# A sequence transform by eight products of 95 rows and 95 columns instead of seven of up to 128 by 377, on one Trainium2 core

## The chip, the cores and the metric

One core of one Trainium2 chip runs the whole program. The metric is the device time of one execution in microseconds (us). Most executions of a kernel agree within 0.3%. A program on one core can show single slow runs; every run quoted here was of the fast state, and the kernel before was run on the same chip in the same rounds as each kernel it is compared with. "Same" means within 2%. Engines: PE is the tensor engine, PEld its weight loads, DVE the vector engine, ACT the scalar engine, POOL is GpSimd.

## The reference

```python
def setup_inputs():            # float32; w_in and w_out reach the kernel as float64
    x = randn(8, 3008, 256) * 0.1
    w_in = randn(256, 2048) / sqrt(256)
    w_out = randn(2048, 256) / sqrt(2048)

def reference(x, w_in, w_out):
    X = np.fft.fft(np.fft.fft(x, axis=1), axis=2).real     # along the sequence (3008), then the features (256)
    h = X.reshape(8 * 3008, 256) @ w_in
    return np.maximum(0.01 * h, h) @ w_out                 # leaky ReLU
```

## The kernel before

The feature transform is folded into w_in, and w_out's seven-product scheme is made once. What remains for each of 8 batches is the sequence transform, then the up-products (`cos_ps`, `sin_ps`), the leaky ReLU and the down-products (`sum_ps`). Frequencies are taken by parity (c = 1 or 0), and each (batch, parity), called a unit, has two parts, cosine and sine. A unit feeds 24 steps, each with four up-products and seven down-products. The folding of x (mirrored rows and columns added and subtracted) runs on DVE. The transform of one part was four products into one bank and three into another, of 95 or 128 rows and 188 to 377 columns:

```python
def even_rows(rows, m, part, c):                 # 4 products of 95 rows
    pe, kf = dft_ps(), KF[c]
    for i in range(NI[0]):
        ... nc.tensor.matmul(to, lhsT=still, rhs=tab[0:PE_ROWS, at : at + to.shape[1]], ...)
def odd_rows(rows, m, part, c):                  # 3 products of 128 rows
    ... nc.tensor.matmul(to, lhsT=still, rhs=tab[:, at : at + to.shape[1]], ...)

def butterfly(t, sums, m, part, c):              # one ACT copy, four DVE operations
    pe, po = sums
    nc.scalar.copy(e0[0:m, 0:kf], pe[0:m, 0:kf])
    nc.vector.tensor_tensor(ev[0:m, 0:kf], e0[0:m, 0:kf], pe[0:m, kf : 2 * kf], op=ALU.add)
    nc.vector.tensor_tensor(ev[0:m, kf:kw], *((x, y), (y, x))[part], op=ALU.subtract)
    nc.vector.tensor_tensor(t[0:m, 0:kw], ev[0:m, 0:kw], po[0:m, 0:kw], op=ALU.add)
    nc.vector.tensor_tensor(t[0:m, kw : UW[c]], ev[0:m, 0:rest], po[0:m, 0:rest], op=ALU.subtract)
```

The start fixes the order of DVE and PE by hand: x of batch 0 comes in four pieces, is folded, transformed, and the first up-products follow, while w_in and w_out are converted from float64 on DVE and ACT. Column d = 128 of x travels apart, as one row of 8 batches ("the d = 128 row", `nyq`). After step 16 the scheduler orders the engines by itself. `keep_warm(n)` issues n products of zeros that only keep the tensor engine busy.

Of the kernel before, what the change touches and what calls it, by code (L numbers as in the profile page):

```python
# [57 lines left out]
NI = [4, 3]  # L59
NT = 7  # L60
PE_ROWS = 95

PO_ROWS = 60
# [4 lines left out]
KF = [189, 188]  # L68
KP = [1, 0]

TW = [[4 * PE_ROWS, 2 * KW[0]], [4 * KF[1], 3 * KW[1]]]
# [12 lines left out]
def m_order(r):  # L84



    at = np.arange(P)[:, None]
    if r == 0:
        m = np.concatenate([2 * at, 2 * at + 1, 376 - 2 * at, 375 - 2 * at], axis=1)  # L90
        last = np.array([188, 187, 190, 189])
        return np.where(at < PE_ROWS - (last != 188), m, -1)
    half = at // (P // 2)
    m = P + at % (P // 2)
    m = np.where(at % (P // 2) < PO_ROWS, np.where(half, 375 - m, m), -1)
    return np.concatenate([at, 375 - at, m], axis=1)


def k_order(c):

    k = 2 * np.arange(KF[c])[::-1] + c
    return np.concatenate([k, Q - k[KP[c] :]])


def laid_out(x):



    m = np.concatenate([m_order(0), m_order(1)], axis=1)
    rows = 2 * m + np.repeat([0, 1], NI)  # L110
    d = np.concatenate([np.arange(P + 1), np.arange(D - 1, P, -1)])
    x = np.concatenate([x, np.zeros((B, 1, D), x.dtype)], axis=1)

    def taken(rows, d):
        return x[:, np.where(m < 0, S, rows % S)][..., d]

    mirrored = (D - d) % D
    x = np.stack([
        np.stack([taken(rows, d), taken(S - rows, mirrored)], axis=2),
        np.stack([taken(H - rows, d), taken(H + rows, mirrored)], axis=2),  # L120
    ], axis=2)
    nyquist = x[..., P].transpose(1, 2, 3, 4, 0).copy()
    x[..., P] = 0.0
    return x, nyquist


def seq_tables():


    out = np.zeros((4, 2, P, TW[1][1]), np.float32)  # L130

    def values(m, r, c):

        s, k = 2 * m + r, k_order(c)
        weight = np.where(m < 0, 0.0, np.where((s == 0) | (s == Q), 0.5, 1.0))[:, :, None]
        turn = (s[:, :, None] * k) % S
# [6 lines left out]
    for r in range(2):  # L143
        for part, t in enumerate(values(m_order(r), r, 1)):
            if r == 0:
                t = t[:, :, : KF[1]]
            out[2 * part + r, 1, :, : TW[1][r]] = t.reshape(P, -1)
    for part, t in enumerate(values(m_order(0), 0, 0)):
        for q in range(2):
            for p in range(2):  # L150
                v = t[:, q, p : KF[0] : 2]
                at = (2 * q + p) * PE_ROWS
                out[2 * part, 0, :, at : at + v.shape[1]] = v

    m = m_order(1)
    m[P // 2 :, 2] = m[: P // 2, 2]
    difference = np.arange(P)[:, None] // (P // 2)
    for part, t in enumerate(values(m, 1, 0)):
        last = t[:, 2] * ((np.arange(KW[0]) + part) % 2 == difference)
        out[2 * part + 1, 0, :, : TW[0][1]] = np.concatenate([t[:, 0, 0::2], t[:, 0, 1::2], last], axis=1)  # L160
    return out

# [28 lines left out]
def columns():  # L191

    at = np.zeros(B * S, np.int64)
    for b, c, j, n, first in chunks()[0]:
        col = j + np.arange(n)
        half = col >= KW[c]
        k = k_order(c)[np.where(half, col - KW[c], col)]
# [7 lines left out]
def tile_fnet_leaky_relu(  # L205
# [6 lines left out]
    seq_tab: bass.AP,  # L212
    feat_tab: bass.AP,
# [29 lines left out]
    def fold_columns(t, h, part, rows):  # L243
# [4 lines left out]
        else:  # L248
            nc.vector.tensor_tensor(z[:, :, P + 1 : D], a[:, :, 1:P], a[:, :, P + 1 : D], op=ALU.subtract)
            nc.gpsimd.memset(z[:, :, P : P + 1], 0.0)  # L250

    def fold_halves(t, part, c, rows, to=None):
# [4 lines left out]
        nc.vector.tensor_tensor(to, z[:, 0], z[:, 1], op=(ALU.add, ALU.subtract)[i])  # L257

    def fold_x(b):
        t, rows = xs.pop(b), slice(0, NT)  # L260
        for h in range(2):
            add_mirrors(t, h, rows)
            for part in range(2):
                fold_columns(t, h, part, rows)
        for part in range(2):
            for c in PARITIES:
                fold_halves(t, part, c, rows)
        zs[b] = t

    def fold_quarters(src, sums, last, tmp):  # L270


        for op, to in zip((ALU.add, ALU.subtract), sums):
            nc.vector.tensor_tensor(to[0:PE_ROWS, 0:2], src[0:PE_ROWS, 0:2], src[0:PE_ROWS, 2:4], op=op)
            nc.vector.tensor_tensor(to[:, 4], src[:, 4], src[:, 5], op=op)
        lo, hi = slice(0, PO_ROWS), slice(P // 2, P // 2 + PO_ROWS)
        nc.scalar.copy(tmp[0][lo], src[hi, 6])
        nc.scalar.copy(tmp[1][hi], src[lo, 6])
        nc.vector.tensor_tensor(last[lo], src[lo, 6], tmp[0][lo], op=ALU.add)
        nc.vector.tensor_tensor(last[hi], tmp[1][hi], src[hi, 6], op=ALU.subtract)  # L280

    def fold_x_quarters(b, part):

        src, z = zs[b][:, part, 0, :, part * P : (part + 1) * P], zs[b][:, part, 1]
        halves = [z[:, :, i * P : (i + 1) * P] for i in range(2)]
        fold_quarters(src, halves, halves[0][:, 5], [h[:, 6] for h in halves])
        quarters[b, part] = halves, halves[0][:, 5]


    folded = {}  # L290
    quarters = {}
# [7 lines left out]
    nyx = const.tile([P, 2, 2, NT, B], F32, name="nyx")  # L299
    inf = const.tile([P, 2], F32, name="inf")  # L300
# [119 lines left out]
    def even_rows(rows, m, part, c):  # L420



        pe, kf = dft_ps(), KF[c]
        tab, n = tabs[2 * part, c], NI[0]
        for i in range(n):
            if c == 1:
                still, to = rows[0:PE_ROWS, i], pe[0:m, i % 2 * kf : (i % 2 + 1) * kf]
            else:
                q, p = divmod(i, 2)  # L430
                still, to = rows[0][(p + part) % 2][0:PE_ROWS, q], pe[0:m, q * kf + p : (q + 1) * kf : 2]
            at = i * TW[c][0] // n

            nc.tensor.matmul(to, lhsT=still, rhs=tab[0:PE_ROWS, at : at + to.shape[1]],  # L434
                             start=(i == 0), stop=(i == n - 1), skip_group_check=True)
        return pe

    def odd_rows(rows, m, part, c):

        po, kw = dft_ps(), KW[c]  # L440
        tab, n, at = tabs[2 * part + 1, c], NI[1], 0
        for i in range(n):
            if c == 1:
                still, to = rows[:, NI[0] + i], po[0:m, 0:kw]
            elif i < 2:
                still, to = rows[0][(i + part) % 2][:, NI[0]], po[0:m, i:kw:2]
            else:
                still, to = rows[1], po[0:m, 0:kw]
            nc.tensor.matmul(to, lhsT=still, rhs=tab[:, at : at + to.shape[1]],  # L449
                             start=(i == 0), stop=(i == n - 1), skip_group_check=True)  # L450
            at += to.shape[1]
        return po

    def butterfly(t, sums, m, part, c):

        pe, po = sums
# [356 lines left out]
```

## Time and profile before

| | before |
|---|---|
| median of three runs | 1931.69 us (1930.21 to 1931.74) |
| span of the profiled run | 1927.9 us |
| PE, DVE, ACT, POOL busy | 99%, 60%, 24%, 55% |
| granted TensorE clock | 1.000 on the mean |

The prediction shows the lines of the page, of the long middle and of single transforms. One more view is needed later: the stretches view of the start, cut where DVE ends the second mix (the sine part's last additions) of the first unit, about where the first sine product begins (28.90 here). Columns: stretch, its length, busy PE, weight loads, DVE, ACT, POOL (with instructions), granted clock, share of the DMA engines, GB/s.

```profile
8.00:28.62 20.62, 18.40 (x86) 12.55 (x85) 17.43 (x32) 4.13 (x11) 2.56 (x7) 1.00 0.82 323
```

DVE worked for 17.43 of the 20.62 us, GpSimd for 2.56, and the clock was full.

### The profile page before, as it was taken

Reading aid. Unit: us, or ns where it says so; the run is one execution under the profiler, and the core shown is the slowest. Engines: PE = TensorE matmul, PEld = TensorE weight load, DVE = VectorE, ACT = ScalarE, POOL = GpSimd, SP = SyncE. Lnnn points to the kernel's source line nnn. Section 1 sums busy time; section 2 is a strip of 40 time slices with the busy share of each in tenths; the row PEclk is TensorE's granted clock in tenths of the full one; section 3 lists DMA queues with packets and bytes.
Section 4 is the critical chain, followed back from the end, with each engine's and each line's share of the span. In section 5 each row is a group of like instructions: output and inputs, shape, how many; then the busy total and the mean of one; then the engine's idle time right before and its main releaser. Section 6 shows DMA issues by size and latency. Waiting matters only on the chain.

```text
span 1927.9 us, 24851 instructions
## 1 busy us (share of the span) xinstructions
PE 1918.2 (99%) x9060; PEld 1694.9 (88%) x9060; DVE 1156.7 (60%) x2276; ACT 468.4 (24%) x554; POOL 1063.3 (55%) x1515
## 2 busy tenths in 40 slices
PE   9999999999999999999999999999999999999999
PEld 7788888888888888888888888888888888888888
DVE  8868555585555755567545765557654585555554
ACT  3532222222222222222222222222222222222221
POOL 1136555575555755566555665556655575555554
PEclk9999999999999999999999999999999999999999
DMA  6202000110002000020000200002000020000000
GB/s 247 77 31 96 12 20 22 52 55 12 21 21 88 19 12 30 12 95 12 22 20 12 95 22 12 20 12 95 23 11 20 12 106 12 19 11 23 11 12 22
DMA packets 26728, 73.29 MB, mean 38 GB/s; under 512 B 4832, under 2 KB 17760, under 8 KB 24816
## 3 DMA queue, kind: packets, MB, share of 16 engines
q1 hardware_dynamic: 25456, 71.71, 10.0%
q8 instruction: 72, 1.18, 0.2%
q14 instruction: 48, 0.39, 0.1%
q10 hardware_dynamic: 1152, 0.00, 0.0%
HBM read 46.99 MB, written 24.71 MB: 37 GB/s over the span
## 4 chain that ended last, share of the span: by engine, by line
PE 97%; DVE 1%; DMA 1%; ACTq 0%; issue 0%; ACT 0%; SPq 0%; DVEq 0%
PE sum_ps L606 57%; PE cos_ps L543 17%; PE sin_ps L543 17%; PE dft_ps L449 3%; PE sum_ps L586 2%; PE dft_ps L434 2%; DMA xt<-in_x_dram 1%; PE wf_ps L396 0%; DMA feat_sb<-in_feat_tab_dram 0%; DVE cos L548 0%; DVE g L552 0%; ACTq L405 0%; DVE g L553 0%; ACT wf L398 0%; DVE power L361 0%
## 5 line engine op out<-in xcount | busy, mean ns | idle before, releaser
L548 DVE SCALAR_TENSOR_TENSOR cos<-nb,wn,cos_ps 128x251 f32<-128x251 f32 (+1 forms) x768 | 330.5, 472 | 674.3 <-PE cos_ps L543 673.8
L554 ACT ACTIVATE g<-g 128x1004 f32<-128x1004 f32 (+1 forms) x384 | 399.2, 1039 | 1191.7 <-DVE g L553 1094.9
L561 POOL TENSOR_TENSOR s<-g 128x251 f32<-128x251 f32 (+1 forms) x368 | 271.5, 738 | 733.7 <-ACT g L554 733.6
L606 PE MATMUL sum_ps<-s,wt 128*128 128x251 f32 (+1 forms) x2208 | 528.0, 374 | 0.0
L606 PEld LDWEIGHTS sum_ps<-s,wt 128*128 128x128 f32 x2208 | 415.5, 188 | 53.1 <-issue 0.6
L543 PE MATMUL cos_ps<-mix,wf 128*128 128x251 f32 (+1 forms) x1536 | 388.3, 375 | 1.8 <-ACT wf L398 1.8
L543 PE MATMUL sin_ps<-mix,wf 128*128 128x251 f32 (+1 forms) x1536 | 387.8, 374 | 0.0
L606 PE MATMUL sum_ps<-g,wo 128*128 128x251 f32 (+1 forms) x1472 | 371.9, 374 | 0.0
L543 PEld LDWEIGHTS cos_ps<-mix,wf 128*128 128x128 f32 x1536 | 290.9, 190 | 37.4 <-ACT wf L398 2.8
L543 PEld LDWEIGHTS sin_ps<-mix,wf 128*128 128x128 f32 x1536 | 290.4, 189 | 34.7
L606 PEld LDWEIGHTS sum_ps<-g,wo 128*128 128x128 f32 x1472 | 279.3, 190 | 39.3 <-DVE o L617 0.3
L564 POOL TENSOR_TENSOR s<-g,s 128x251 f32<-128x251 f32 (+1 forms) x368 | 272.5, 741 | 28.9
L552 DVE TENSOR_TENSOR g<-cos,sin_ps 128x502 f32<-128x502 f32 (+1 forms) x384 | 259.7, 676 | 47.4 <-DVE cos L548 12.2
L562 POOL TENSOR_TENSOR s<-s,g 128x251 f32<-128x251 f32 (+1 forms) x368 | 275.5, 749 | 0.0
L563 POOL TENSOR_TENSOR s<-g 128x251 f32<-128x251 f32 (+1 forms) x368 | 260.4, 708 | 0.0
L553 DVE TENSOR_TENSOR g<-cos,sin_ps 128x502 f32<-128x502 f32 (+1 forms) x384 | 257.2, 670 | 0.0
L606 PE MATMUL sum_ps<-s,wo 128*128 128x251 f32 (+1 forms) x736 | 215.8, 375 | 0.0
L606 PE MATMUL sum_ps<-g,wt 128*128 128x251 f32 (+1 forms) x736 | 215.8, 375 | 0.0
L606 PEld LDWEIGHTS sum_ps<-s,wo 128*128 128x128 f32 x736 | 139.5, 189 | 16.3
L606 PEld LDWEIGHTS sum_ps<-g,wt 128*128 128x128 f32 x736 | 139.8, 190 | 15.8
L617 DVE TENSOR_TENSOR o<-e,sum_ps 128x251 f32<-128x251 f32 (+1 forms) x184 | 67.4, 408 | 8.7 <-ACT e L615 8.7
L586 PE MATMUL sum_ps<-g,wo 128*128 128x251 f32 x256 | 57.4, 375 | 0.0
(75 smaller groups left out, 680.8 us busy)
## 6 DMA issues: line engine op xcount, KB each, us to landing
xt<-in_x_dram SPq DMA_DIRECT2D x14, 1792.0 KB, 9.0
out_dram<-o SPq DMA_DIRECT2D x80, 251.0 KB, 2.3
raw<-in_w_out_dram SPq DMA_DIRECT2D x8, 512.0 KB, 4.6
out_dram<-o SPq DMA_DIRECT2D x16, 250.0 KB, 2.1
raw<-in_w_in_dram SPq DMA_DIRECT2D x6, 512.0 KB, 4.7
nb<-nyq_dram SPq DMA_DIRECT2D x8, 376.5 KB, 3.3
nb<-nyq_dram SPq DMA_DIRECT2D x7, 376.0 KB
xt<-in_x_dram SPq DMA_DIRECT2D x2, 1024.0 KB, 9.5
```

The costliest lines, as they stand in the source:

```text
L543: nc.tensor.matmul(pt[blk][:, h * n : (h + 1) * n], lhsT=wf[:, blk, fs[h] * P : (fs[h] + 1) * P], rhs=mixed[b, c][blk][:, at : at + n], st ...
L548: nc.vector.scalar_tensor_tensor(cos[:, hs], in0=spreads[b, c][:, at : at + n], scalar=wn[:, fs[h] : fs[h] + 1], in1=pt[0][:, hs], op0=ALU ...
L552: nc.vector.tensor_tensor(g[:, 0], cos[:, 0 : 2 * n], pt[1][:, 0 : 2 * n], op=ALU.add)
L553: nc.vector.tensor_tensor(g[:, 1], cos[:, 0 : 2 * n], pt[1][:, 0 : 2 * n], op=ALU.subtract)
L554: nc.scalar.activation(g, g, ACT.Lrelu)
L561: nc.gpsimd.tensor_tensor(s1, a[1][0], a[1][1], op=ALU.add)
L562: nc.gpsimd.tensor_tensor(s2, s1, a[0][0], op=ALU.subtract)
L563: nc.gpsimd.tensor_tensor(s3, a[0][0], a[1][0], op=ALU.subtract)
L564: nc.gpsimd.tensor_tensor(s4, a[0][1], s2, op=ALU.subtract)
L586: nc.tensor.matmul(sums[j][d][:, r * n : (r + 1) * n], lhsT=wo[:, fs[h] // NH, fs[h] % NH, d * P : (d + 1) * P], rhs=a[r][h], start=(f == ...
L606: nc.tensor.matmul(sums[j][p], lhsT=still[p], rhs=moving[p], start=(f == 0 and i % 2 == 0), stop=(f == NH - 1), skip_group_check=True)
L617: nc.vector.tensor_tensor(to, x, y, op=ALU.add)
```

## The change

The intent is to hold the tensor engine for a shorter time in each transform. Rows of x are sorted into eight chunks of 95 instead of seven of up to 128. Some chunks are first *turned*: pairs of rows are combined with a cosine and a sine (ACT makes two scaled copies, DVE two scalar_tensor_tensor operations, or ACT four copies and GpSimd two additions). After that eight products of 95 rows and some 95 columns give what seven wider ones gave, and a longer *butterfly* (nine operations and two ACT copies instead of four and one) puts the frequencies together. The d = 128 row's butterfly in the start goes to GpSimd, and so do the sine's last folds and turns. x is folded in two halves per batch instead of one. The core of the diff:

```diff
-NI = [4, 3]
-NT = 7
-PE_ROWS = 95
-PO_ROWS = 60
+NI = [4, 4]
+NT = 8
+ROWS = 95
@@
-    def fold_x(b):
+    def fold_x(b, h):
...
+    def turn(x, y, a, part, tmp, to, v):
+        nc.scalar.activation(tmp[0], y, ACT.Copy, scale=sin)
+        nc.scalar.activation(tmp[1], y, ACT.Copy, scale=cos)
+        if v is nc.vector:
+            v.scalar_tensor_tensor(to[0], in0=x, scalar=cos, in1=tmp[0], op0=ALU.mult, op1=op[part])
+            v.scalar_tensor_tensor(to[1], in0=x, scalar=sin, in1=tmp[1], op0=ALU.mult, op1=op[1 - part])
+            return
+        ...                                      # on GpSimd: two more ACT copies, two additions
@@ 
+    def products(stills, to, tab, bank):         # four products into one bank, twice a part
+        for i, (still, o) in enumerate(zip(stills, to)):
+            nc.tensor.matmul(o, lhsT=still, rhs=moving, start=(i == 0), stop=(i == 3), skip_group_check=True)
@@
-    def butterfly(t, sums, m, part, c):
+    def butterfly(to, m, part, c, v=nc.vector):  # parity 1: five operations in even, four in odd
...
@@ steps
-                    if n % 2 == 1:
-                        fold_x(b + 1)
+                if part == 0 and n % 2 == 1 and f in (2, 5):
+                    fold_x(b + 1, f // 5)
@@ start
+            fold_columns(t, 0, 1, evens, nc.gpsimd)
+            nyq = mix_nyquist(nyq, nc.gpsimd)
...
+            cosine.fold_even()
+            sine.fold_even(nc.gpsimd)
...
+            even, odd = mix(units[0], 0)
+            even(even_cosines)
+            fold_halves(t, 1, 1, odds, v=nc.gpsimd)
+            sine.fold_odd(nc.gpsimd)
+            odd_cosines = odd_rows(cosine, P)
+            odd(odd_cosines)
+            spread_first(nyq)
+            even, odd = mix(units[0], 1)
+            even(even_sines)
+            odd(odd_rows(sine, P))
             o.begin()
             o.mantissa()
-            mix(units[0], 1, sums_of_sines)
```

## The prediction

> **What bounds the kernel now.** I read the page first, then the stretches view, then the tensor engine's timelines around single transforms, and the timeline of the first 35 us last. The page and its chain of work that ended last:
>
> ```profile
> PE 1918.2 (99%) x9060; PEld 1694.9 (88%) x9060; DVE 1156.7 (60%) x2276; ACT 468.4 (24%) x554; POOL 1063.3 (55%) x1515
> ...
> PE 97%; DVE 1%; DMA 1%; ACTq 0%; issue 0%; ACT 0%; SPq 0%; DVEq 0%
> PE sum_ps L606 57%; PE cos_ps L543 17%; PE sin_ps L543 17%; PE dft_ps L449 3%; PE sum_ps L586 2%; PE dft_ps L434 2%; DMA xt<-in_x_dram 1%; PE wf_ps L396 0%; DMA feat_sb<-in_feat_tab_dram 0%; DVE cos L548 0%; DVE g L552 0%; ACTq L405 0%; DVE g L553 0%; ACT wf L398 0%; DVE power L361 0%
> ```
>
> The tensor engine is on 97% of the chain, and the transform that the change rewrites (dft_ps, L434 and L449) is only 5% of it as rounded. Busy PE alone proves little, since its ends are modelled, so I look at the long middle by itself:
>
> ```profile
> 200.00:1900.00 1700.00, 1700.00 (x8064) 1511.87 (x8063) 990.27 (x1948) 393.75 (x445) 987.41 (x1407) 1.00 0.08 30
> ```
>
> Columns: length, then busy PE, weight loads, DVE, ACT, POOL, granted clock, DMA share, GB/s. In 1700 us the tensor engine never stands still, DVE and POOL have 42% to spare, DMA 92%. Whatever time the transform's products take there is paid in full; what DVE, ACT, POOL and DMA do is hidden. So the measure of the change is: how long is the tensor engine held by one part (one unit, cosine or sine) before and after. Starts of successive groups tell it, not busy times. First a part of parity 1, then one of parity 0, both PE:
>
> ```profile
> 259.77 1.44 PE L434 MATMUL dft_ps<-tab,xt 95*128 95x188 f32 x8
> 261.04 2.06 PE L449 MATMUL dft_ps<-tab,xt 128*128 128x376 f32 x6
> 262.94 1.01 PE L606 MATMUL sum_ps<-g,wo 128*128 128x251 f32 x4
> ```
>
> ```profile
> 146.79 1.03 PE L434 MATMUL dft_ps<-tab,xt 95*128 95x95 f32 x8
> 147.66 1.47 PE L449 MATMUL dft_ps<-tab,xt 128*128 128x189 f32 x6
> ```
>
> Every f32 product leaves two records (x8 is four products, x6 is three). Parity 1 holds the engine from 259.77 to 262.94, 3.17 us. Parity 0 starts at 146.79 and the next product of another kind starts at 148.96: 2.17 us. The wide products show the price of a column: six records of 376 in 1.90 us, 317 ns each, 0.84 ns per column and record. The narrow ones break that price: 8 records of 95 columns should take 8 x 80 ns = 0.64 us, and took 0.87 us (109 ns each). The weight-load row and a warming group of 126 columns say why:
>
> ```profile
> 11.66 2.19 PEld L651 LDWEIGHTS sum_ps<-blank 128*128 128x128 f32 x18
> ```
>
> Eighteen loads of about 0.19 us each in 2.19 us: one starts every (2.19 - 0.19)/17 = 0.118 us on the average, and their matmuls (126 columns, 18 in 2.17 us, the last 0.275) every (2.17 - 0.275)/17 = 0.111 us. A product of 128 stationary columns is thus never nearer than 0.112 us a record to the next, however few columns it moves. The counter-case is the d = 128 row at 120.92 us: the same 95 columns but 8 stationary ones run 8 records in 0.67 us, 84 ns each, which is the column price.
>
> **What the Trainium skill says.** "TensorE: Matmul & The Clock Gate", section "LDWEIGHTS (loading the stationary operand)": a load lasts P/1.2 ns, P being its columns and not the rows of the contraction; 128 columns give 107 ns. The trace agrees with the pace (112 ns, with 95 rows as with 128), not with the recorded duration (190 ns, loads overlap). The same page, "Back-to-back issue gap": in a stream of load and matmul pairs both set the spacing. Agreed, as above. "VectorE: DVE Perf Modes", section "The TRN2 errata": an fp32 tensor_tensor takes (N+151)/0.96 ns. The trace has 0.54 us for 376 columns, 0.41 for 256, 0.28 for 128: agreed, and small operations are mostly fixed cost. "SBUF — State Buffer", "Who interferes with whom": a DVE tensor_tensor with two SBUF inputs shuts GpSimd out for its whole length. The trace agrees: one GpSimd addition at 156.45 us took 2.17 us beside a 2.02 us DVE addition of 1792 columns, others 0.63.
>
> **The change, part by part.**
>
> *Tensor engine.* A part of parity 1 had 4 x 188 + 3 x 376 = 1880 columns in 7 products; it gets 380 + 378 = 758 in 8. Parity 0 had 378 + 754 = 1132 in 7; it gets 380 + 382 = 762 in 8. By columns (2 x 0.84 ns) the new part would take 1.28 us. I do not take that: all its products have 94 to 96 columns and 128 stationary ones, so 16 records x 0.112 = 1.79 us holds. Parity 1 saves 3.17 - 1.79 = 1.38 us, parity 0 saves 2.17 - 1.79 = 0.38. Batches 1 to 7 of parity 1 (14 parts; batch 0 lies in the start) give 14 x 1.38 = 19.3; 16 parts of parity 0 give 16 x 0.38 = 6.1; the d = 128 row of parity 0, 8 stationary columns, goes from 2.03 us (120.92 to 122.95) to 16 x 0.084 = 1.34, 0.7. Sum **26.1 us**. The dft_ps share of the chain should fall from 4.4% to about 3.1%.
>
> *DVE.* Per batch now: from the groups, folding of x 14.3 us (2 x 2.04, 4 x 1.26, 4 x 1.30), quarters 5.0, butterflies 57.1/8 = 7.1; 26.4. After, with the (N+151)/0.96 that the trace bears out: folding 8/7 as much, 16.3; rows 32 operations of 128 or 256 columns, 10.4; butterflies nine operations a part instead of four, 1880 and 1507 columns, 2 x (3.4 + 3.0) = 12.8. Sum 39.5: 13 us more per batch, about 105 us in all, DVE busy 60% to some 66%. The fold of x, one 14 us lump before, now comes as two halves, which the instruction order shows spread one operation per step between the evacuations. Hidden.
>
> *ACT.* 16 scaled copies and some more evacuations per batch, some 8 us each batch, ACT 24% to 28%. Hidden. *GpSimd:* only the start's folds, hidden later. *DMA:* x is 8/7 as large, tables less than half; DMA is idle in the middle. Hidden.
>
> *The start.* Before, the last piece of x is folded from 18.60 us, and the first real up-product begins at 27.95, sines at 28.90:
>
> ```profile
> 18.60 0.96 DVE L241 TENSOR_TENSOR xt<-xt 128x768 f32<-128x768 f32 x1 [0.30 <-DMA xt<-in_x_dram]
> ...
> 27.95 1.11 PE L543 MATMUL cos_ps<-mix,wf 128*128 128x251 f32 x4
> ```
>
> Bytes ahead of the last piece: before 0.52 (w) + 0.26 (feature table) + 0.11 + 3.67 (x) + 0.96 (two tables) = 5.5 MB; after 0.52 + 0.13 + 4.19 + 0.39 = 5.2. At the 343 GB/s of the first 20 us it lands some 0.8 us sooner, 17.8. Then, in the order that the instruction listing gives: DVE 1.23 + 0.69 + 0.79 to 20.5; ACT's first scaled copies and four DVE turns 1.5, to 22.0; two sums of 256, 0.8; eight products 1.8; a copy 0.3, to 24.9; odd cosines 1.8 to 26.7; sines 1.5 + 1.8 to 30.0, against 28.6 before. So the first sine product comes about 1.4 us later, and the first conversion of w_out, three operations that ran between the two mixes, now comes after them. From 20 to 80 us DVE is 17 to 18 us busy of each 20 and the tensor engine waits about 3 us in all, so a later DVE can cost it. I charge **+1.5 us** (0 to 4).
>
> Time: 1931.7 - 26.1 + 1.5 = **1907 us**, 1.3% faster.
>
> **Rivals.**
> 1. *The column count rules.* Then a part takes 1.28 us and the saving is 14 x 1.89 + 16 x 0.89 + 0.7 = 41 us: 1892, just over 2%. Against it stand the 0.109 and 0.111 us of two groups of 95 and 126 columns.
> 2. *DVE becomes a bound in places.* It gains 13 us a batch in more and smaller operations that wait for ACT and for each other, and the two transform banks come from the same four as the up-products. If the evacuation is late, PE waits. For it: DVE at 66%, and steps where a fold fills the 4.66 us of a step. Against it: before, a 14 us fold cost nothing, and the sums wait three steps behind. If each of 30 parts cost 0.5 us, 1922.
> 3. *GpSimd is shut out longer* by the added SBUF additions and its sums come late. It has 42% spare and some 8 us of lead, so I expect 0 to 3 us.
> 4. *The start gets worse or better* by several us: more links between DVE, ACT, PE and GpSimd, against a shorter first load. 1903 to 1912.
>
> **Range and chances.** The 26 us rest on a measured pace, with 1 to 2 us of doubt at joints between groups; the start has 3 either way; rivals 2 and 3 only lengthen. So 1900 to 1916. Over 2% faster needs 1894 or less: only rival 1, or a start 13 us shorter than I think, 6%. Slower by 2% would take a stall of 60 us, 1%.
>
> **What would show it.** Right: 16 records per part spaced 0.112 us, a transform every 1.8 us for both parities, PE without idle time from 200 to 1900 us, DVE near 66%, the first up-product at 27 to 30 us. Wrong: records at 80 to 90 ns (rival 1); gaps of PE before up-products ended by DVE evacuations of dft_ps or cos_ps (rival 2), or before sum_ps ended by GpSimd (rival 3); PE gaps before 130 us that differ by more than 4 us from the kernel before (rival 4).

## The result and the profile after

| | before | after |
|---|---|---|
| median (four runs each) | 1930.95 us (1929.78 to 1931.74) | 1920.22 us (1919.46 to 1921.36) |
| span of the profiled run | 1927.9 us | 1917.6 us |

The ratio is 0.9945 (95% interval 0.9928 to 0.9963): "same", 0.55% faster. Here and below a ratio is the mean time of one kernel's fast runs over the mean of the other's fast runs of the same rounds, so it is not quite the ratio of the medians. The prediction took off 24.6 us (26.1 less 1.5); about 10 came.

The page of the kernel after, busy times and the chain of work that ended last:

```profile
PE 1898.6 (99%) x9132; PEld 1689.9 (88%) x9132; DVE 1293.5 (67%) x2580; ACT 514.1 (27%) x721; POOL 1136.7 (59%) x1551
...
PE 92%; DVE 4%; issue 1%; DMA 0%; ACTq 0%; ACT 0%; DVEq 0%; SPq 0%
```

DVE at 67% and ACT at 27% are what was predicted (66% and 28%). But PE carries only 92% of the chain instead of 97%, and DVE 4% instead of 1%: in several places the end of the program now hangs on DVE. First, the transform itself, on PE's timeline around one part (start, busy us, engine, line, operation, tiles, shapes, count):

```profile
228.37 1.92 PE L524 MATMUL dft_ps<-tab,xt 95*128 95x95 f32 x16
230.13 1.04 PE L735 MATMUL sum_ps<-g,wo 128*128 128x251 f32 x4
```

From 228.37 to 230.13 is 1.76 us for 16 records, 0.110 us each, where 1.79 were predicted and 3.17 or 2.17 were held before. So the saving is there: 14 x (3.17 - 1.76) + 14 x (2.17 - 1.76) = 25.5 us for the 28 parts of the middle. The stretches view of the middle shows the first leak:

```profile
200.00:1900.00 1700.00, 1696.24 (x8212) 1517.97 (x8211) 1125.52 (x2253) 430.86 (x567) 1049.29 (x1425) 1.00 0.08 32
400.00:800.00 400.00, 398.99 (x1928) 356.74 (x1927) 272.61 (x542) 104.28 (x141) 254.59 (x339) 1.00 0.08 28
```

PE was busy for all 1700 us before; now it misses 3.8 by this view, in six waits in five of the batches, all ended by DVE's L746. (Starts will show 5.4 us below: PE's ends are modelled and hide the first part of each wait.) One such place on PE's timeline, and DVE's timeline in front of it; the brackets name the idle time before a group and what ended it:

```profile
648.64 1.04 PE L735 MATMUL sum_ps<-g,wo 128*128 128x251 f32 x4
650.45 1.09 PE L735 MATMUL sum_ps<-s,wt 128*128 128x251 f32 x4 [0.76 <-DVE e L746]
```

```profile
645.26 1.76 DVE L280 TENSOR_TENSOR xt<-xt 128x1024 f32<-128x1024 f32 x1
...
648.11 0.40 DVE L746 TENSOR_TENSOR o<-e,sum_ps 128x250 f32<-128x250 f32 x1
648.44 0.40 DVE L746 TENSOR_TENSOR e<-e,sum_ps 128x250 f32<-128x250 f32 x1
648.76 1.21 DVE L280 TENSOR_TENSOR xt<-xt 128x1024 f32<-128x1024 f32 x1
649.90 0.73 DVE L746 TENSOR_TENSOR e<-e,sum_ps 128x250 f32<-128x250 f32 x2
```

L746 empties the banks in which the next chunk's down-products begin. L280, the fold of the next batch's x, is nobody's hurry, but it stands between the L746 operations in DVE's queue, 1.21 us long, and PE waits for the one behind it.

The second leak is the start. The stretches view up to the end of DVE's second mix:

```profile
8.00:38.94 30.94, 22.92 (x94) 17.24 (x93) 23.51 (x40) 9.57 (x31) 20.81 (x35) 0.73 0.53 197
20.00:40.00 20.00, 13.28 (x41) 9.57 (x40) 17.65 (x34) 7.77 (x25) 9.69 (x18) 0.59 0.25 81
```

DVE ended that mix at 38.94 instead of 28.62 (the sine product, at 38.63, waited only for its first half). DVE was busy 6.1 us longer (23.51 against 17.43) and stood idle 4.2 us longer; GpSimd worked 20.81 us instead of 2.56; from 20 to 40 us the granted clock was 0.59. DVE's timeline shows where the 10 us arise:

```profile
15.24 1.06 DVE L280 TENSOR_TENSOR differences<-xt 128x512 f32<-128x512 f32 x1
...
19.93 0.69 DVE L280 TENSOR_TENSOR xt<-xt 128x512 f32<-128x512 f32 x1 [1.91 <-POOL xt L273]
20.54 1.22 DVE L264 TENSOR_TENSOR xt<-xt 128x1024 f32<-128x1024 f32 x1
21.79 0.93 DVE L270 TENSOR_TENSOR xt<-xt 128x512 f32<-128x512 f32 x1
22.64 0.93 DVE L272 TENSOR_TENSOR xt<-xt 128x508 f32<-128x508 f32 x1
23.50 1.21 DVE L264 TENSOR_TENSOR xt<-xt 128x1024 f32<-128x1024 f32 x1
24.75 0.69 DVE L270 TENSOR_TENSOR xt<-xt 128x512 f32<-128x512 f32 x1
25.47 1.63 DVE L280 TENSOR_TENSOR differences<-xt 128x512 f32<-128x512 f32 x1
27.57 0.80 DVE L301 SCALAR_TENSOR_TENSOR folded<-differences,angle,folded 95x128 f32<-95x128 f32 x1 [0.47 <-ACT folded L298]
```

The last piece of x is folded from 23.50, not from 17.8, and no bracket there names a DMA: DVE came late, not the data. One operation of 512 columns takes 0.69 us at 19.93 and 1.06 or 1.63 at 15.24 and 25.47, where GpSimd has additions of its own. The wait of 1.91 us is for a memset of four values, which stood in GpSimd's queue behind the d = 128 butterfly. The first up-product begins at 36.52 instead of 27.95.

To follow this shift I read from PE's timeline where the first up-product of the k-th step starts (384 steps: 16 units of 24), "the k-th up-product" for short:

| up-product | before | after | later by |
|---|---|---|---|
| 1st | 27.95 | 36.52 | 8.6 |
| 3rd | 40.68 | 51.89 | 11.2 |
| 16th | 114.16 | 125.39 | 11.2 |
| 25th | 161.21 | 170.75 | 9.5 |
| last (384th) | 1909.86 | 1899.56 | -10.3 |

From the 3rd to the 16th the two kernels run in step, 11.2 us apart. So whatever happens up to the 3rd up-product is paid in full. One caution for what follows: each kernel has one profile, and the first piece of x, for which DVE waits, is folded from 8.9 to 9.9 us in the profiles of this study (9.66 before, 9.01 after). Differences under about one us between two profiles' starts are not settled.

### The profile page after: what moved, and what is told of

The parts are those of the page before. It is cut to its first block, busy times and chain, and to the rows that moved or that the text cites. A ratio compares the mean times of both kernels' runs of the same rounds, so it can differ in the third digit from the quotient of the medians.

```text
span 1917.6 us, 25461 instructions
## 1 busy us (share of the span) xinstructions
PE 1898.6 (99%) x9132; PEld 1689.9 (88%) x9132; DVE 1293.5 (67%) x2580; ACT 514.1 (27%) x721; POOL 1136.7 (59%) x1551
## 3 DMA queue, kind: packets, MB, share of 16 engines
q1 hardware_dynamic: 25600, 74.40, 10.4%
## 4 chain that ended last, share of the span: by engine, by line
PE 92%; DVE 4%; issue 1%; DMA 0%; ACTq 0%; ACT 0%; DVEq 0%; SPq 0%
PE sum_ps L735 54%; PE cos_ps L672 16%; PE sin_ps L672 16%; PE dft_ps L524 3%; PE sum_ps L715 2%; DVE g L681 1%; DVE cos L677 1%; DVE g L682 1%; DVE xt L280 1%; DVE xt L272 0%; DMA xt<-in_x_dram 0%; PE wf_ps L468 0%; DVE xt L264 0%; DVE e L746 0%; ACTq L477 0%
## 5 line engine op out<-in xcount | busy, mean ns | idle before, releaser
L691 POOL TENSOR_TENSOR s<-s,g 128x251 f32<-128x251 f32 (+1 forms) x368 | 318.6, 866 | 0.0
L693 POOL TENSOR_TENSOR s<-g,s 128x251 f32<-128x251 f32 (+1 forms) x368 | 279.7, 760 | 28.9
L746 DVE TENSOR_TENSOR o<-e,sum_ps 128x251 f32<-128x251 f32 (+1 forms) x184 | 67.4, 408 | 8.7 <-ACT e L744 8.7
L524 PEld LDWEIGHTS dft_ps<-tab,xt 95*128 95x128 f32 x484 | 59.2, 192 | 1.6
```

The source lines that it names most:

```text
L524: nc.tensor.matmul(o, lhsT=still, rhs=moving, start=(i == 0), stop=(i == 3), skip_group_check=True)
L691: nc.gpsimd.tensor_tensor(s2, s1, a[0][0], op=ALU.subtract)
L693: nc.gpsimd.tensor_tensor(s4, a[0][1], s2, op=ALU.subtract)
L746: nc.vector.tensor_tensor(to, x, y, op=ALU.add)
```

## The experiments

Names used in the expectations. CLOCK: the tensor engine's halved clock makes the start long. CHAIN: DVE's waits in the start, above all the one for GpSimd's memset, do. PORT: GpSimd's added operations stretch DVE's. OWN WORK: the added operations themselves, by their number, fill DVE's queue. DVE ORDER: the scheduler's order of DVE makes the gaps of the middle. Other names are explained in the expectation that brings them. All kernels are the one after with small edits; a kernel that computes wrong results on purpose is marked, and all others gave correct results.

### 1. The wait for the memset

```diff
             v.tensor_tensor(z[:, :, P + 1 : D], a[:, :, 1:P], a[:, :, P + 1 : D], op=ALU.subtract)
-            nc.gpsimd.memset(z[:, :, P : P + 1], 0.0)
```

> The changed kernel without GpSimd's zeroing of column 128 of the folded rows (the host already sends zeros there, so results stay right). Question: why does the first up-product start at 36.5 us instead of 28. Theory CHAIN (DVE's folding of the first batch is held up, by GpSimd's queue among others): the 1.9 us that DVE waited for GpSimd at 18.0 us disappear, the first up-product starts near 34.5, the whole is about 2 us shorter. Theory CLOCK (the tensor engine runs at half clock from 18.6 to 42.5 us and that makes the start long): no change, within 0.5 us.

Measured: 1918.69 us (1917.73 to 1918.83), ratio to before 0.9935 (0.9918 to 0.9951). The first up-product came at 37.70, 1.2 us *later* (x itself began 0.5 later in this profile); that the median is 1.5 us below after's in spite of it comes from the middle. The wait of 1.91 us is gone, but DVE now ran beside more of GpSimd's work. DVE's timeline of this run:

```profile
24.16 2.45 DVE L270 TENSOR_TENSOR xt<-xt 128x512 f32<-128x512 f32 x1
```

The same operation took 0.69 us at 24.75 above. The wait was not a cost by itself: taken away, it came back as longer operations and the start got no shorter.

### 2. The clock

```diff
-            keep_warm(8)
+            keep_warm(12)
             even_cosines = even_rows(cosine, P)
...
+            keep_warm(4)
             even_sines = even_rows(sine, P)
+            keep_warm(12)
```

> The changed kernel with more warming products on zeros where the tensor engine stood idle in the start (12 instead of 8, then 4 and 12 more). Theory CLOCK: the granted clock stays 1.0 from 18 to 42 us and the first up-product starts by 31 us, the whole is 8 us or more shorter. Theory CHAIN: the clock stays 1.0, but the folding of DVE ends at 29.9 us as before, so the first up-product starts at 35 to 36 us, later ones gain what half clock cost after it: 2 to 4 us in all.

Measured: 1918.90 us (1917.50 to 1919.46), ratio 0.9936 (0.9921 to 0.9951). From 20 to 40 us the granted clock rose from 0.59 to 0.85, and the products of the cosines and of the d = 128 row ran at full speed; the first up-product came at 37.35, not sooner. PE's timeline tells why:

```profile
30.60 1.15 PE L524 MATMUL dft_ps<-tab,folded 95*128 95x95 f32 x8 [1.02 <-ACT wf L470]
31.68 1.53 PE L650 MATMUL dft_ps<-nyq,one 1*128 1x376 f32 x4
35.54 2.02 PE L524 MATMUL dft_ps<-tab,folded 95*128 95x95 f32 x8 [2.33 <-POOL folded L338]
```

The faster PE waits 2.33 us for the folded sine rows from GpSimd. In that wait its clock falls to half again (0.50 from 34 to 40 us), so this run tests a full clock only up to about 34 us: that is worth nothing here by itself, since DVE's and GpSimd's rows come no sooner. (x began 0.8 us later in this profile, as much as the up-product did.) The half clock that stayed holds the odd sines for 2.02 us instead of 1.10 at full clock (experiment 12), so some 0.9 us of CLOCK stay untested here.

### 3. Both together

The edits of 1 and 2 (with `keep_warm` 12, 4 and 8).

> Both edits, no zeroing by GpSimd and warming products (12, 4, 8). CHAIN: the two gains add up, 4 to 6 us shorter than the changed kernel, first up-product at 33 to 34.5 us. CLOCK: the same as with warming alone, 8 us or more.

Measured: 1918.42 us (1915.84 to 1921.37), ratio 0.9935 (0.9920 to 0.9950), first up-product at 37.49. Neither CLOCK nor CHAIN brought what it promised, nor did their sum; here too PE waited for GpSimd's sine rows (2.71 us) and ran at half clock from there on.

### 4. The order of the vector engine in the middle

The fold of x is cut into six pieces, one in each of six steps, and DVE and PE keep the program's order from step 16 on.

```diff
-                if part == 0 and n % 2 == 1 and f in (2, 5):
-                    fold_x(b + 1, f // 5)
+                if n % 2 == 1 and 3 <= part * NH + f <= 8:
+                    fold_x(b + 1, part * NH + f - 3)
@@
-    for at in range(16, len(steps) + lag):
-        step(at)
+    with tc.manual_schedule(engines={mybir.EngineType.DVE, mybir.EngineType.PE}):
+        for at in range(16, len(steps) + lag):
+            step(at)
```

> The changed kernel, from step 16 on with DVE and the tensor engine in program order, and the folding of the next batch in six pieces, one a step, clear of the step in which the sums of a finished block are read out. Question: what are the gaps of the tensor engine of about 1 us per batch (5.3 us from 200 to 1900 us). Theory DVE ORDER (the fold of x stands in DVE's queue before and between the additions that free the sum banks): the gaps fall below 1 us in all, the whole is 4 to 6 us shorter. Rival (GpSimd's sums late because DVE shuts it out, or the banks of the transform): the gaps stay within 1 us of what they were or move to another wait, no gain over 1.5 us.

Measured: 1914.76 us (1914.21 to 1915.27), ratio 0.9916 (0.9901 to 0.9931). The same stretch of the middle:

```profile
200.00:1900.00 1700.00, 1700.00 (x8238) 1524.67 (x8237) 1139.48 (x2267) 433.76 (x580) 1016.33 (x1431) 1.00 0.08 32
```

PE is full again, the profile ends at 1912.4 instead of 1917.6, 5.1 us sooner, and the start is unchanged (1st up-product 36.69, 25th 171.06). DVE did slightly more work in the stretch, so it was order and not load. DVE ORDER is confirmed. The run makes two edits at once, six pieces and the fixed order; neither was tried alone, so which of the two does it is not shown.

### 5. The d = 128 butterfly on DVE

```diff
-            nyq = mix_nyquist(nyq, nc.gpsimd)
...
             odd(odd_cosines)
-            spread_first(nyq)
+            spread_first(mix_nyquist(nyq, nc.vector, nyq_tile))
```

> The first four runs threw out both earlier theories of the start (without the wait for GpSimd DVE's operations only got longer; at full clock the first up-product was no sooner). New theory PORT: in the start DVE is the path, and DVE additions of two SBUF inputs and GpSimd's operations shut each other out, so work given to GpSimd is paid on DVE as waiting. Here the butterfly of the d = 128 row (nine GpSimd additions, 12 to 20 us) goes to DVE, after the odd cosines. PORT: DVE ends the folding of the cosines (29.9 us in the changed kernel) 3 to 5 us sooner, pays the nine operations (about 3 us) later, first up-product 34 to 36 us, whole 0 to 3 us shorter. Rival OWN WORK (DVE's own greater work is the whole delay): the folding ends at 29.9 as before, everything 3 us later.

Measured: 1922.13 us (1921.68 to 1923.80), ratio 0.9958 (0.9943 to 0.9973); first up-product at 39.70, 3.2 us later. The time is what OWN WORK said, the way there is not: the cosine rows were folded at 27.27 and not at 29.9, 2.7 us sooner, near what PORT said. The edit lost this again, since DVE now did the butterfly after the odd cosines, from 32.32 to 35.43, with PE waiting for it, and then waited 3.29 us itself for the odd sines. PE's timeline:

```profile
35.12 2.84 PE L651 MATMUL dft_ps<-nyq,one 1*128 1x376 f32 x4 [3.48 <-DVE nyq L582]
37.89 2.02 PE L524 MATMUL dft_ps<-tab,folded 95*128 95x95 f32 x8
```

So the run decides between neither.

### 6. Everything of the first unit on DVE

The edits of 1 and 5, all folds and turns of the start on DVE, and products that keep the clock (10, 4, 6).

> All folding of the first batch and the d = 128 butterfly on DVE, GpSimd's zeroing gone, warming products (10, 4, 6). PORT: although DVE gets some 8 us more work, its operations keep their undisturbed lengths (0.69 us for 512 columns), the folding of the cosines ends by 27 us, first up-product at 32 to 36, whole 1 to 4 us shorter than the changed kernel. OWN WORK: 5 to 8 us longer.

Measured: 1924.30 us (1924.12 to 1925.20), ratio 0.9969 (0.9954 to 0.9984), first up-product at 41.19. GpSimd is now almost idle and no DVE operation is stretched, yet the start is 4.7 us longer: moving the work to these places in DVE's queue costs more than the stretching did. It does not refute PORT: the cosine rows were folded at 27.37, 2.6 us sooner than in the kernel after, about as PORT said (27). Then, as in 5, the d = 128 butterfly lay in the way, on DVE from 33.85 to 36.92, and PE waited 5.28 us for it. The time came near OWN WORK's range (5 to 8 us longer) without its mechanism being shown.

### 7. The d = 128 butterfly left out

*Wrong results on purpose (relative error 0.046).* Two ACT copies stand in for GpSimd's nine additions.

```diff
-            nyq = mix_nyquist(nyq, nc.gpsimd)
+            nc.scalar.copy(nyq[0:B, 0:380], banks[0][0:B, 0:380])
+            nc.scalar.copy(nyq[0:B, 376 : UW[1]], banks[1][0:B, 0:376])
```

> Wrong results on purpose: the nine GpSimd additions of the d = 128 row are left out in the start (two ACT copies fill the tile), nothing else moves. It measures what those nine cost DVE. PORT: the wait at 18 us and the stretched operations of 17 to 24 us go, folding of the cosines ends 3 to 5 us sooner (25 to 27 us), the whole is 3 to 5 us shorter. OWN WORK: less than 1.5 us, DVE goes through its own queue as before.

Measured: 1914.65 us (1913.44 to 1916.12), ratio 0.9919 (0.9902 to 0.9935). The start is 3.2 us shorter at the 1st up-product and 3.4 at the 25th; the other 1.8 us come in the middle, where the gaps of DVE's order fell otherwise. Nine additions of 8 rows on GpSimd, an engine that had idle time before, cost the program 3.4 us. That is inside PORT's 3 to 5 us and above OWN WORK's 1.5; the cosine rows were folded at 26.71 (PORT: 25 to 27) instead of 29.94, although two operations stayed stretched (1.63 and 0.80 us). As the memset's wait taken away alone (experiment 1) gave nothing, it is GpSimd's work that counts here, by the port and by its queue, and the run does not part these two.

### 8 to 10. One cause at a time, then all

Built on the kernel of experiment 4, so that the middle does not blur the end. *All three give wrong results on purpose.* Experiment 8 uses before's four operations in the first unit's two butterflies:

```diff
+                if quick:                        # in the first unit only
+                    v.tensor_tensor(ev[0:m, 0:188], e0[0:m, 0:188], pe[0:m, 190:378], op=ALU.add)
+                    either(ev[0:m, 188:376], e0[0:m, 0:188], pe[0:m, 190:378])
+                    return
...
+                if quick:
+                    v.tensor_tensor(to[0:m, 0:kw], ev[0:m, 0:kw], po[0:m, 0:kw], op=ALU.add)
+                    v.tensor_tensor(to[0:m, kw : UW[c]], ev[0:m, 0:kw], po[0:m, 0:kw], op=ALU.subtract)
+                    return
```

> Built on the spread kernel (1914.8 us, first up-product of the trace at 36.69, the 25th at 171.06, end 1912.44). Wrong results on purpose: in the first unit's two mixes each nine-operation butterfly is replaced by the four operations of before, reading the banks as they are. OWN WORK theory (the start is bound by the vector engine's and GpSimd's own added operations): two times 3.4 us of operations become two times 1.8, so the start is 3 to 4.5 us shorter, 25th up-product near 167, end near 1909. Rival (the start waits for the last part of x and for the sine's chain through ACT and GpSimd; the butterflies lie beside it): 0 to 1.5 us shorter.

Experiment 9 leaves out the first unit's turns:

```diff
+            if self.turnless:
+                self.even = [self.src[:, i] for i in (0, 2, 1, 3)]
...
+            if self.turnless:
+                v.tensor_tensor(z(12, 2), x, y, op=ALU.add)
+                v.tensor_tensor(z(14, 2), x, y, op=ALU.subtract)
```

> Built on the spread kernel. Wrong results on purpose: the first unit's rows are not turned (no scaled copies on ACT, no scalar_tensor_tensor on the vector engine, no additions of turned rows on GpSimd); the sums of the odd rows stay. OWN WORK: six operations of 0.35 us and two waits of 0.47 us leave the vector engine's queue and GpSimd loses six additions of 0.45 to 0.9: the start is 3 to 4 us shorter, 25th up-product near 167.5. Rival (data of x arrives late and sets the start): 0 to 1.5 us.

Experiment 10 does 7, 8 and 9 together:

> Built on the spread kernel. Wrong results on purpose: no d = 128 butterfly on GpSimd, four-operation butterflies and no turns, in the first unit alone. OWN WORK: 3.4 + 3.5 + 3.5 = about 10 us, so the first up-product stands near 27 to 28.5 and the 25th near 161, as in the kernel before the change (27.95 and 161.21); end near 1902.5. Rival (something else of the change, such as the order of the loads or the clock, is a good part of the later start): a rest of 3 us or more stays, 25th up-product at 164 or later.

| | time, us | ratio | 1st up-product | 3rd | 25th |
|---|---|---|---|---|---|
| 4, the base | 1914.76 | 0.9916 | 36.69 | 51.91 | 171.06 |
| 8, four operations | 1913.48 (1913.00 to 1913.78) | 0.9913 | 36.58 | 50.91 | 170.05 |
| 9, no turns | 1913.12 (1912.70 to 1913.34) | 0.9912 | 35.39 | 50.60 | 169.76 |
| 10, all three | 1907.95 (1906.31 to 1908.47) | 0.9884 | 30.94 | 45.14 | 164.62 |
| before, same rounds | 1929.83 (1929.10 to 1931.22) | 1 | 27.95 | 40.68 | 161.21 |

Single removals gave 1.0 and 1.3 us where 3 to 4 were expected: OWN WORK as a sum of DVE's durations failed, and its rivals' numbers (0 to 1.5 us) came true in both. In 9, what DVE saved in operations it waited instead: the wait for the memset behind GpSimd's butterfly grew from 1.91 to 3.62 us. In 8, DVE waited for PE and ACT instead. All three together gave 6.4 us at the 25th up-product, a little more than their parts (3.4 of experiment 7, 1.0 and 1.3). Another 3.4 us were left, as the expectation's rival had it (25th at 164 or later), but not from late data: DVE's timeline of experiment 10 shows the last piece folded as soon as DVE is done with the one before, with no DMA in a bracket.

```profile
18.27 0.68 DVE L272 TENSOR_TENSOR xt<-xt 128x508 f32<-128x508 f32 x1
18.87 1.22 DVE L264 TENSOR_TENSOR xt<-xt 128x1024 f32<-128x1024 f32 x1
```

PE's timeline of experiment 10 shows a new bound:

```profile
22.22 1.86 PE L533 MATMUL dft_ps<-tab,xt 95*128 95x95 f32 x8
24.04 2.37 PE L533 MATMUL dft_ps<-tab,folded 95*128 95x95 f32 x8
26.33 2.87 PE L667 MATMUL dft_ps<-nyq,one 1*128 1x376 f32 x4
29.13 2.02 PE L533 MATMUL dft_ps<-tab,folded 95*128 95x95 f32 x8
30.94 1.94 PE L689 MATMUL cos_ps<-mix,wf 128*128 128x251 f32 x4
```

PE works nearly without a stop, at half clock: from start to start, the first and the last eight records of a transform here take 1.8 us that took 0.9 in the middle (the second eight 2.3).

### 11. The clock, once the other work is gone

*Wrong results on purpose.* Experiment 10 with seven products of zeros ahead of the fold of w_in and ten, then (12) four, after the even sines.

> Wrong results on purpose: the kernel without d = 128 butterfly, turns and nine-operation butterflies in the first unit (1908.0 us; first up-product at 30.94, third at 45.14, 25th at 164.62), plus 17 products that keep the tensor engine busy where it waited. There the tensor engine worked without a stop from 22.2 to 35.6 us at half its clock. PARALLEL CHAINS theory (the start is the longest of a vector engine chain, a GpSimd chain and a tensor engine chain at half clock, within a few us of each other; taking one away bares the next): with the clock granted in full, its products from 22 to 36 us lose up to 5 us, the first up-product stands at 27.5 to 29, the third at 40.5 to 42.5 as in the kernel before (27.95, 40.68), the 25th at 160.5 to 162. Rival (the rest of 3.4 us at the 25th is a later arrival of data or the order of the loads): the 25th stays at 164 or later.

With ten: 1907.54 us (1907.12 to 1908.08), ratio 0.9883 (0.9866 to 0.9899), clock 1.00 throughout, 1st up-product at 31.08 and 25th at 164.92: no gain. This run was a bad test. Its ten products end at 27.68, 2.1 us after DVE had the cosine rows ready, so they themselves stood in the way. That its rival's number (164 or later) came true therefore says nothing about the clock.

> As k15_three_warm (wrong results on purpose), but with four instead of ten products after the even sines: there the ten ended 2.2 us after the folded cosine rows were ready, so that run could not tell the clock. PARALLEL CHAINS: with the clock granted in full and no added product in the way, the odd cosines run at 25.5, the first up-product at 28.5 to 29.3, the third at 43 to 44 (45.14 at half clock), the 25th at 162.3 to 163.3 (164.62). If the half clock costs nothing here either: 164.3 or later.

With four: 1904.88 us (1904.74 to 1904.88), ratio 0.9865 (0.9850 to 0.9880). The starts came a little sooner than expected. PE's timeline of this run, which ends the search for causes:

```profile
24.12 1.40 PE L533 MATMUL dft_ps<-tab,folded 95*128 95x95 f32 x8
25.45 1.52 PE L667 MATMUL dft_ps<-nyq,one 1*128 1x376 f32 x4
26.96 1.10 PE L533 MATMUL dft_ps<-tab,folded 95*128 95x95 f32 x8
27.89 1.72 PE L689 MATMUL cos_ps<-mix,wf 128*128 128x251 f32 x4
```

The 1st up-product is at 27.89 (before the change 27.95), the 3rd at 42.27 (40.68) and the 25th at 161.72 (161.21). The clock that was worth nothing alone is worth 2.9 us here, although it fell to half again from about 28 to 31 us (the line at 27.89). With the four causes gone (the d = 128 butterfly, the longer butterflies, the turns, the clock) the later start is gone but for 1.6 us at the 3rd and 0.5 us at the 25th. Where the 1.6 us lie is best seen in experiment 11 with ten products, whose clock stayed full; PE's timeline, at the first down-products:

```profile
37.95 5.34 PE L732 MATMUL sum_ps<-g,wo 128*128 128x251 f32 x24 [1.52 <-DVE wo L443]
```

PE waits 1.52 us there for DVE's conversion of w_out; before the change, the same products (at 32.88) waited for nothing. In experiment 12 they begin at 34.76, and the slower up-products leave 0.30 us of the wait to be seen.

### 13. GpSimd's folds beside DVE's

*Wrong results on purpose.* Experiment 12 without GpSimd's folding of the last sine rows.

```diff
-                fold_columns(t, h, 1, odds, (nc.vector, nc.gpsimd)[h])
+                if h == 0:
+                    fold_columns(t, h, 1, odds)
...
-            fold_halves(t, 1, 1, odds, v=nc.gpsimd)
-            sine.fold_odd(nc.gpsimd)
+            sine.odd = [sine.src[:, i] for i in range(4, 8)]
```

> As k17_three_warm4, and GpSimd's four folding operations of the last sine rows are left out as well (wrong results on purpose), so that nothing of GpSimd's stands beside the vector engine's last folds, which took 1.63, 1.38 and 0.94 us for 0.69, 0.42 and 0.42. SHARED PORT: the vector engine ends the folding 2.4 us sooner, the third up-product at 40.7 to 41.8 (before the change: 40.68) and the 25th at 160 to 161.5 (before: 161.21), so that the list of causes is closed. If the stretched operations wait for data and not for GpSimd: third at 43 or later, as k17.

Measured: 1904.99 us (1904.81 to 1905.12), ratio 0.9866 (0.9851 to 0.9881), 3rd up-product at 42.23: no gain, and a miss by both expectations (40.7 to 41.8, or 43). Yet DVE did get faster. DVE's timeline of experiment 12, then of this one:

```profile
20.66 1.63 DVE L280 TENSOR_TENSOR differences<-xt 128x512 f32<-128x512 f32 x1
22.32 1.37 DVE L340 TENSOR_TENSOR folded<-differences 95x256 f32<-95x256 f32 x1
23.62 0.94 DVE L341 TENSOR_TENSOR folded<-differences 95x256 f32<-95x256 f32 x1
```

```profile
21.01 0.69 DVE L280 TENSOR_TENSOR differences<-xt 128x512 f32<-128x512 f32 x1
21.73 0.46 DVE L340 TENSOR_TENSOR folded<-differences 95x256 f32<-95x256 f32 x1
22.12 0.41 DVE L341 TENSOR_TENSOR folded<-differences 95x256 f32<-95x256 f32 x1
```

The three operations took 3.94 us beside GpSimd and 1.56 without it, so the stretching is GpSimd's doing. But PE reached the odd cosines only at 24.47, behind my products of zeros, and DVE then waited 2.12 us for it. The time does not show what the stretching costs once it is the last of the causes; that stays open.

### 14 to 16. Correct kernels that try to use this

Split: experiment 4 without the memset, and of the d = 128 butterfly the five even operations on DVE, where it waits for x at 11 to 12.6 us, the four odd ones on GpSimd.

```diff
-            nyq = mix_nyquist(nyq, nc.gpsimd)
+            nyq = mix_nyquist(nyq, nc.vector, nc.gpsimd)     # even part, odd part
```

> Correct results; a candidate to beat both kernels: the spread fold of x, no memset of column 128, and in the start the d = 128 row's five even operations on the vector engine, where it waits for x at 11 to 12.6 us, the four odd ones on GpSimd. OWN WORK with a shared port: the vector engine loses its wait of 1.9 us and some stretched operations and gains 1.7 us partly in an idle stretch: 1 to 2.5 us shorter than the spread kernel's 1914.8, so 1912.5 to 1914. If the total of work of the two engines alone counts: 0 to 1.

Measured: 1913.35 us (1913.24 to 1913.97), ratio 0.9914 (0.9899 to 0.9928), profile 1911.5, 25th up-product at 170.08, 1.0 sooner than in 4 (x began 0.3 us sooner in its profile). It met its range. This is the fastest correct kernel of the study; its lead over 4 is one us of the profile, and the intervals of the two ratios overlap.

Split and clock: also DVE's mirrors of the odd rows ahead of the first turn, and `keep_warm` of 12, 4, 14 and 7.

> Correct results; the candidate to beat both: the spread fold of x, no memset, the d = 128 row split between the vector engine and GpSimd, the mirrors of the odd rows ahead of the first turn, and products that keep the clock. PARALLEL CHAINS: the sine's chain over GpSimd still sets the first up-product, so 0 to 2 us below the split kernel (1913.4): 1911.5 to 1913.4. Rival (the clock costs by itself what its half rate takes, some 3 us from 29 to 42): 1910 or less.

Measured: 1916.07 us (1915.99 to 1917.24), ratio 0.9929 (0.9914 to 0.9944), 1st up-product 38.44, clock 1.00. Slower than both expectations: the 14 products of zeros end at 32.03, and DVE had folded the cosine rows by 30.06; the next 7 end at 37.57, and GpSimd had folded the sine rows by 34.83. Both edits went in together, so which share is whose stays open.

Split and conversion: the three operations that begin the conversion of w_out go between the halves of the first butterfly, into a wait of 0.9 us on DVE.

```diff
             even(even_cosines)
+            o.begin()
+            o.mantissa()
...
-            o.begin()
-            o.mantissa()
```

> Correct results: the split kernel (1913.4; third up-product at 50.93), with the three vector operations that begin the conversion of w_out put between the two halves of the first cosine butterfly, where the vector engine waits 0.9 us, instead of behind the sines. VECTOR QUEUE theory (up to the third up-product the sum of the vector engine's work and waits sets the time): 0.5 to 1.0 us sooner, 1912.4 to 1912.9. If the chain over GpSimd and the tensor engine to the first up-product sets it: 0.3 to 0.6 us later.

Measured: 1916.69 us (1915.56 to 1916.75), ratio 0.9924 (0.9908 to 0.9941), 3rd up-product at 54.38, 3.4 us later. A miss by both theories. ACT's order in the start is the program's as well, and two ACT operations of the conversion now stood ahead of the sine's scaled copies:

```profile
31.71 0.72 ACT L418 ACTIVATE power<-power,inf 128x512 f32<-128x512 int32 x1 [2.19 <-DVE power L417]
...
33.09 0.39 ACT L299 ACTIVATE folded<-xt,angle 95x128 f32<-95x128 f32 x1
```

ACT waited 2.19 us for DVE's result, and the sine's copies began at 33.09 instead of 28.95.

## Why the prediction was wrong

The prediction was 1907 us, 1900 to 1916; it came to 1920. "Same" was right, the range was not.

| step of the prediction | predicted | measured |
|---|---|---|
| pace of the new products | 1.79 us a part | 1.76 us a part |
| saving behind the 25th up-product (26.1 less 2 x 0.38 and 0.7) | 24.6 us | 25.3 us with DVE in order (experiment 4) |
| saving between the 16th and the 25th | 1.5 us | 1.7 us |
| gaps of PE in the middle ("Hidden") | 0 | 5.4 us |
| the start | +1.5 us (0 to 4) | +11.2 us |
| sum | -24.6 us | -10.4 us |

The measured rows are differences of up-product starts: behind the 25th, before took 1927.91 - 161.21 = 1766.70 us, experiment 4 took 1912.44 - 171.06 = 1741.38, after took 1917.56 - 170.75 = 1746.81. So the gaps are 1746.81 - 1741.38 = 5.4, and the sum is 11.2 - 1.7 - 25.3 + 5.4 = -10.4 us, the difference of the two profiles.

**Right:** the step that mattered most, that the 0.112 us of a product with 128 stationary columns, and not the columns, sets the price. Rival 1 (the column count, 41 us) fell. DVE's and ACT's shares of the span were near too (66% and 28% predicted, 67% and 27% measured), though DVE's added work came to 137 us where 105 were reckoned, and ACT's to 46 where 64 were.

Two readings in it are a little off, without harm to the sum: "never nearer than 0.112 us" beside its own groups at 0.109 and 0.111 (0.110 came), and DVE's "17 to 18 us busy of each 20", which is 16.5 to 18.1. And the pace was measured for loads of 128 columns and moves of about 95 to 126; for wider moves the columns set the price, as its own 376-column group shows.

**Wrong, step "DVE ... Hidden".** The prediction said of the fold that "a 14 us fold cost nothing" before and that the order listing "shows spread one operation per step between the evacuations". It did stand between the evacuations, and that was the harm: 1.2 to 1.8 us of fold in front of the additions that free the sum banks. Rival 2 named the mechanism, but at the evacuation of the transform and the up-products. It came at L746, where the wait "three steps behind" gives no slack, since a new chunk takes the banks that the last one has just filled. It was also left out of the sum, although named: 42% of idle DVE says nothing of the microsecond in which PE needs it. GpSimd (rival 3) worked 62 us longer in the stretch from 200 to 1900 (1049 against 987 us) with nearly the same number of instructions, but ended none of these waits.

**Wrong, step "The start", mis-sized by 9.7 us.** The prediction laid one chain from the arrival of the last piece of x at 17.8 us and took DVE to be free there. No trace gives the arrival exactly, but in experiment 10 DVE folds this piece from 18.87 without any wait, so the data were there by then. DVE came at 23.50 because it and GpSimd were still busy with the earlier pieces: 5.7 us after the predicted 17.8, at least 4.6 after the data. The fold then took 3.6 instead of 2.7 us (L280 1.63 instead of 0.69 beside GpSimd), and the rest of the chain 2.0 us more than laid out, so that the first sine product came at 38.63 and not at 30.0. Of GpSimd the prediction wrote "only the start's folds, hidden later". In the start nothing is hidden: GpSimd's d = 128 butterfly alone cost 3.4 us (experiment 7).

**What the prediction did not think of** is the clock: in the kernel after the clock records show half speed from 18.6 to 22.0 us and again from 25.4, in PE's wait of 6.2 us for the cosine rows, until 42.5 us. By itself a full clock up to 34 us gains nothing (experiment 2), because DVE's and GpSimd's chain is the longer one. With that shortened, it is worth 2.9 us (10 against 12). The start is the longest of several chains through DVE, GpSimd, ACT and PE that lie within a few us of each other. That is why each cause removed alone gave 0 to 3.4 us, and all together 9.3 of 9.9 (171.06 - 161.72, of 171.06 - 161.21). The split of the 9.9 us into shares depends on the order in which they are removed; only the sum is settled. What is left, 1.6 us at the 3rd up-product, is seen as PE's wait for the first conversion of w_out (1.52 us in experiment 11), which came between the two mixes before and follows them now; the one run that moved it (16, split and conversion) failed for another reason, so no run shows that moving it takes the 1.6 us away.

## What to carry to other kernels

Price short products by the load of their stationary columns and not by the columns that they move: this held to 2%. When an engine with 40% to spare gets more work, ask which of its operations somebody waits for and what now stands in front of them in the queue; here two lumps of background work in the scheduler's order cost 5 us, and six small ones in the program's fixed order cost nothing. And a start that runs once is a set of chains in parallel: predict it as an order of all engines, and test causes together, since one cause removed alone uncovers the next.

## What the Trainium skill lacked or had wrong

- "SBUF — State Buffer", section "Who interferes with whom": the rule held, and the traces add sizes. A DVE addition of 512 columns with two inputs in SBUF took 0.69 us alone and up to 2.45 us beside GpSimd's additions; three DVE operations took 3.94 us beside GpSimd and 1.56 without. A scalar_tensor_tensor was stretched too, 0.80 against 0.34 us: the section's rule for two SBUF inputs covers it, its list of operations doesn't name it.
- "TensorE: Matmul & The Clock Gate", section "LDWEIGHTS (loading the stationary operand)", gives P/1.2 ns (107 for 128 columns) without a word on the clock's state. Eight records with 128 stationary columns took 0.9 us from start to start at full clock (0.110 each in the middle) and 1.8 us at half clock (experiment 10), about 0.23 each: the pace of the loads halves as well. And nothing there warns that products issued to keep the clock can delay the waiting work themselves: ten of them, of 256 columns, took 4.5 us and used up the gain.
- No page that I read has a measured time for additions as small as these on GpSimd, or for what DVE beside them does to it: additions of 8 rows and 94 to 376 columns took 0.5 to 1.35 us each there in the kernel after (0.51 for 188 columns while DVE stood idle); on DVE (experiment 6) those of 94 to 188 columns took 0.23 to 0.34 us.
